# Earlier places for the second batch's keys, queries and values, and the strided heads' buffer as two tiles: one Trainium2 kernel, one change

## The chip, the cores and the metric

One core of one Trainium2 chip runs the whole program. The metric is the device time of one execution in microseconds, as the median of several runs. Beside it there is one profiled execution, from which all views below come. Engines: PE (matrix products), DVE and POOL (elementwise), ACT (activations and copies), SP (here it only issues transfers).

## The reference

Eight batches, eight heads, 576 positions, head size 64. Heads 0 to 3 see the last 32 positions; heads 4 to 7 see the earlier positions of the same residue modulo 32. Then a low-rank mix over the positions (U, V of rank 32) and a two-layer block with a ReLU:

```
scores = scale * q @ k.T ; masked by (0 <= i-j < 32) for heads 0-3,
                           by (i >= j and i % 32 == j % 32) for heads 4-7
attn   = softmax(scores) ; x = concat_heads(attn @ v)          # [8, 576, 512]
u      = x + (x.T @ U @ V).T
out    = u + relu(u @ w_ch1) @ w_ch2                           # 512 -> 2048 -> 512
```

U, V, w_ch1 and w_ch2 arrive as 64-bit floats.

## The kernel before

The two layers run as nine blocks of 512 columns (eight batches of 512 positions each, and one block of the eight remainders of 64). Each block has 16 steps (`fc`), each with 12 matmuls of 128x512 of the first layer (`gemm1`, L431) and 12 of the second (`gemm2`, L449): every float32 operand is split in a high and a low part (`uh`, `ul`; `gh`, `gl`; two halves of each weight `w`), and three of the four products are made. `gh` is made on ACT (L437), `gl` on DVE (L438).

The 64-bit weights come as 32 pieces (`raw`) and are converted while the first block runs. I call one piece a chunk: ACT L84, then DVE L86, L87 and L89, then ACT L112, then POOL L113.

Batch 0's attention runs ahead of the first block (`first_attention`). Beside block n runs the attention of batch n+1, step by step, after a plan with due times (`plan`, `tick`). Batches 0 and 1 do all eight heads on PE, as four pairs of heads; from batch 2 on, two pairs are on PE and the four strided heads run on POOL and DVE (`strided_heads`, tile `st`: queries in one half, keys and later values in the other).

One pair (`attention_pair`) is: scores (L143, L149 on PE), maximum and difference (DVE L157, L158), exp (ACT L161), transposes (PE L171), copy to `PT` (ACT L174), outputs (PE L182), normalisation (DVE L191 to L201: for a local pair its last piece is L196, for a strided pair L201). Then `mix_t` (PE L319, L323; ACT L326; DVE L328), `u_strided_early` (PE L386 and L359), `u_local` (L367, L359) and `u_tail` (L397, L359). From the first block on, all of these take their PSUM from one pool with one buffer, `px`:

```
    def psx2():
        banks["n"] += 1
        if banks["prefix"] and banks["n"] % 3:
            return ps_acc.tile([128, 2, 512], F32, name="acc")
        return ps_x.tile([128, 2, 512], F32, name="px")
```

Keys and queries (`kT`, `qT`) lie in the pool `att` of seven buffers, which `cv` (chunks), `s_sb`, `PT` and others share; values lie in one buffer `vt`. The code gives an order of emission; a scheduler then decides each engine's order with its own estimates of time, and every engine works through its own order strictly. All transfers go through SP's queue, where each waits for the one eight places ahead of it.

Of the kernel before, what the change touches and what calls it, by code (L numbers as in the profile page):

```python
# [7 lines left out]
F32 = mybir.dt.float32  # L8
# [10 lines left out]
NCH = S // 32  # L19
# [7 lines left out]
STAGGER = 3  # L27
ATT_BUFS = 7
PAIR_ORDER = (0, 2, 3, 1)
CHUNK_ORDER = ((2, 3, 0, 1), (0, 1, 2, 3))  # L30


@with_exitstack
def fused_kernel(ctx, tc, lqk, lv, eqk, ev, sqkv, U, V, wts, masks, eye, out):
# [10 lines left out]
    def att(shape, name, dtype=F32):  # L45
        return ap_.tile(shape, dtype, name=name, tag="att", bufs=ATT_BUFS)
# [11 lines left out]
    def dma(out, in_):  # L58
        last_dma[0] = nc.sync.dma_start(out=out, in_=in_).ins
# [35 lines left out]
    def load_weights(n):  # L95
        while wl["loaded"] < min(n, len(chunks)):
            k = wl["loaded"]
            c = chunks[k]
            raws[c] = const.tile([128, 512], I64, name="raw%d_%d_%d" % c, tag=wtag(*c))
            with tc.issue_after(last_dma[0]):  # L100
                dma(out=raws[c], in_=wts[k])
            wl["loaded"] += 1
# [12 lines left out]

    Vp = ap_.tile([96, S], F32R, name="Vp", tag="st")
    raw_u = att([128, 320], "raw_u", I64)
    raw_v = ap_.tile([32, S], I64, name="raw_v", tag="vt")  # L120

# [119 lines left out]
    o_str = {}  # L241

    def strided_heads(b):
        st = ap_.tile([128, 2, NCH * D], F32, name="st", tag="st")
        sq, sk = (st[:, x].rearrange("p (i d) -> p i d", d=D) for x in range(2))
        dma(out=st[:, 0], in_=sqkv[b - NSP, 0])
        dma(out=st[:, 1], in_=sqkv[b - NSP, 1])
        yield
        s_st = ap_.tile([128, NCH, NCH], F32, name="s_st")
        nc.gpsimd.memset(s_st, 8.0 * NEG)  # L250
        late = []

        def flush(n):
            while len(late) > n:
                late.pop(0)()

        for i in range(NCH):
            for j0 in range(0, i + 1, 9):
                n = min(9, i + 1 - j0)
                tmp = att([128, 9, D], "tmp")  # L260
                nc.gpsimd.tensor_tensor(out=tmp[:, 0:n], in0=sk[:, j0:j0 + n], in1=sq[:, i:i + 1].broadcast_to([128, n, D]),  # L261
                                        op=ALU.mult)
                late.append(lambda tmp=tmp, n=n, i=i, j0=j0: nc.vector.tensor_reduce(  # L263
                    out=s_st[:, i, j0:j0 + n], in_=tmp[:, 0:n], axis=AX.X, op=ALU.add))
                flush(1)
                yield
        flush(0)
        sv = sk
        dma(out=st[:, 1], in_=sqkv[b - NSP, 2])
        yield  # L270
        m_st = ap_.tile([128, NCH], F32, name="m_st")
        nc.vector.tensor_reduce(out=m_st, in_=s_st, axis=AX.X, op=ALU.max)
        nc.vector.tensor_tensor(out=s_st, in0=s_st, in1=m_st.broadcast_to([128, NCH, NCH]), op=ALU.subtract)
        nc.scalar.activation(out=s_st, in_=s_st, func=AF.Exp, scale=0.125)
        yield
        yield
        nc.vector.tensor_reduce(out=m_st, in_=s_st, axis=AX.X, op=ALU.add)
        nc.vector.tensor_scalar(out=m_st, in0=m_st, scalar1=1e-9, scalar2=None, op0=ALU.add)
        nc.vector.reciprocal(out=m_st, in_=m_st)
        nc.vector.tensor_tensor(out=s_st, in0=s_st, in1=m_st.broadcast_to([128, NCH, NCH]), op=ALU.mult)  # L280
        yield
        for i in range(NCH):
            step = D if i < 9 else D // 2
            for d0 in range(0, D, step):
                tmp = att([128, (i + 1) * step], "tmp")
                tv = tmp.rearrange("p (j d) -> p j d", d=step)
                nc.gpsimd.tensor_tensor(out=tv, in0=sv[:, 0:i + 1, d0:d0 + step],  # L287
                                        in1=s_st[:, i, 0:i + 1].broadcast_to([128, i + 1, step]), op=ALU.mult)
                late.append(lambda tv=tv, i=i, d0=d0, step=step: nc.vector.tensor_reduce(  # L289
                    out=sq[:, i, d0:d0 + step], in_=tv.rearrange("p j d -> p d j"), axis=AX.X, op=ALU.add))  # L290
                flush(1)
                yield
        flush(0)
        yield
        xT = st[:, 1].rearrange("p (e s) -> p e s", e=2)
        nc.vector.transpose(out=xT.rearrange("p e (i r) -> p i e r", r=32), in_=sq.rearrange("p i (e x) -> p i e x", x=32))
        o_str[b] = xT
        yield
        for h in range(4):
            rows = slice(32 * h, 32 * h + 32)  # L300
            xh = x_str.rearrange("p t (e h x) -> p t h e x", e=2, h=4)[:, :, h]
            oh = sq[rows].rearrange("p i (e x) -> p i e x", e=2)
            for i4 in range(4):
                nc.scalar.copy(out=xh[32 * i4:32 * i4 + 32, 0:4], in_=oh[:, i4:16:4])  # L304
                if i4 % 2:
                    yield
            for i4 in range(2):
                nc.scalar.copy(out=xh[32 * i4:32 * i4 + 32, 4], in_=oh[:, 16 + i4])
            yield
# [174 lines left out]
    def run_staggered(gens, lag):  # L484
        live, waiting, n = [], list(gens), 0
        while live or waiting:
# [5 lines left out]
                    live.remove(g)  # L492
            yield

    def first_attention():
        scratch = [up.tile([128, NDC * TB], F32, name="scr", tag=t) for t in ("uh", "ul")]
        late = [const.tile([128, 9, D + 1], F32, name=f"ve{n}", tag=wtag(n // 4, 3, n % 4)) for n in range(8)]
        loads = {}

        def load(k):  # L500
            pr = PAIR_ORDER[k]
            if k < 3:
                qk = [scratch[j // 3][:, S * (j % 3):S * (j % 3) + S] for j in (2 * k, 2 * k + 1)]
            else:
                qk = [att([128, S], "kT"), att([128, S], "qT")]
            loads[k] = pair_loads(0, pr, (*qk, late[2 * k], late[2 * k + 1]))

        load(0)
        dma(out=masks_sb, in_=masks)
        dma(out=ident, in_=eye)  # L510
        load(1)
        load(2)
        small_loads()
        load(3)
        load_weights(24)
        nc.gpsimd.memset(x_loc[64:128, 4], 0.0)
        nc.gpsimd.memset(x_str[64:128, 4], 0.0)
        pairs = [attention_pair(0, pr, loads[k]) for k, pr in enumerate(PAIR_ORDER)]
        beside = {3: lambda: (small_u(), small_v()), 4: lambda: convert(2)}
        seen = 0  # L520
        steps = run_staggered(pairs, STAGGER)

        def go(n):
            nonlocal seen
            for _ in range(n):
                if next(steps, "end") == "end":
                    return
                if len(exps) > seen:
                    seen = len(exps)
                    beside.get(seen, lambda: None)()  # L530

        go(3 * STAGGER + 8)
        mix_t(0, 1)
        go(2)
        u_strided_early(0, 2)
        go(40)
        mix_t(0, 0)
        u_strided_early(0, 3)
        for dc in range(2):
            u_local(0, (dc,))  # L540
        convert(5)

    first_attention()
    banks["prefix"] = False
    load_weights(32)
    pend = []
    c0 = wl["conv"]

# [5 lines left out]
    def task(gen, key, start, rate=1.0, after=()):  # L554
        return [gen, key, start, rate, after, 0.0]
# [6 lines left out]
    def plan(n):  # L562
        b = n + 1
        if n == 0:
            return [
                task(calls(lambda: u_tail(0)), "tail0", 2),
                task(run_staggered([attention_pair(1, pr) for pr in (2, 3, 0, 1)], 7), "pairs", 2, 1.0),
                task(calls(lambda: mix_t(1, 1), lambda: mix_t(1, 0)), "mix", 30, 0.4, ("pairs",)),
                task(calls(lambda: u_strided_early(1, 2), lambda: u_strided_early(1, 3), lambda: u_local(1, (0, 1)),
                           lambda: u_tail(1)), "u", 38, 0.34, ("mix",)),  # L570
            ]
        if b < B:
            return [
                task(strided_heads(b), "str", 0, 1.5),
                task(run_staggered([attention_pair(b, 0), attention_pair(b, 1)], 5), "pairs", 0, 1.0),
                task(calls(lambda: mix_t(b, 0)), "mix0", 20, 1.0, ("pairs",)),
                task(calls(lambda: u_local(b, (0, 1))), "u0", 26, 1.0, ("mix0",)),
                task(calls(lambda: mix_t(b, 1)), "mix1", 47, 1.0, ("str",)),
                task(calls(lambda: u_strided(b), lambda: None, lambda: None, lambda: u_tail(b)), "u1", 53, 1.0, ("mix1", "u0")),
            ]  # L580
        if b == B:
            return [task(u_rest(), "rest", 12)]
        return []
# [116 lines left out]
```

## Time and profile before

| what | us |
|---|---|
| median of 3 runs | 953.71 |
| lowest and highest | 951.01, 954.39 |
| the profiled execution | 954.11 |
| its span in the trace | 952.3 |
| PE, DVE, ACT, POOL busy | 917.1, 536.9, 247.3, 403.4 |

The time of the profiled execution is 1.8 us above the span of its trace. In the profile, L431 is line 431 of the kernel before; in the kernel after the change the lines up to 480 stand two further down (L431 is L433, L182 is L184). A row of a timeline has the start, the length, the engine, the line, the operation, output <- inputs, and in brackets the idle time before it with what ended it. Matmuls overlap, so the lengths of two neighbours add up to more than the time that they take.

### The profile page before, as it was taken

To read this page: it belongs to the slowest core of one execution; us is meant where nothing else is said; L and a number is where in the kernel's file an instruction comes from. 1 tells how busy PE (TensorE), PEld (TensorE's weight loads), DVE (VectorE), ACT (ScalarE), POOL (GpSimd) and SP (SyncE) were. 2 spreads that over 40 slices of the span, in tenths; PEclk is the share of its full clock that TensorE was granted. 3 is DMA by queue.
4 is the path that set the end of the run, shared out by engine and by line. 5 is a ranking of instruction groups with operands and counts; after the bars stand their busy time and mean duration, and the time that the engine had idled before them with its cause. 6 is when DMAs were issued, how large, how long until landed. Compare 5 with 4: busy or idle time off the path is not lost.

```text
span 952.3 us, 16503 instructions
## 1 busy us (share of the span) xinstructions
PE 917.1 (96%) x6896; PEld 725.8 (76%) x6896; DVE 536.9 (56%) x912; ACT 247.3 (26%) x486; POOL 403.4 (42%) x407
## 2 busy tenths in 40 slices
PE   5789898999999999999999999999999999999998
PEld 3557566878787787778778878787778788888886
DVE  4686778548936693659465964597448831112112
ACT  2443345212421142114311341115112521111110
POOL 0142233565639471939185816763575530002000
PEclk9989998999999999999999999999999999999999
DMA  9962202111022101220122003110210020001001
GB/s 338 408 259 67 77 27 75 45 57 52 25 79 71 52 26 56 70 76 5 41 105 77 1 25 119 33 51 26 95 56 26 1 80 15 1 1 45 1 1 44
DMA packets 27098, 64.50 MB, mean 68 GB/s; under 512 B 6768, under 2 KB 7280, under 8 KB 27024
## 3 DMA queue, kind: packets, MB, share of 16 engines
q1 hardware_dynamic: 27024, 63.45, 19.2%
q8 instruction: 54, 0.88, 0.4%
q14 instruction: 20, 0.16, 0.1%
HBM read 52.96 MB, written 10.49 MB: 67 GB/s over the span
## 4 chain that ended last, share of the span: by engine, by line
PE 79%; issue 9%; DVE 4%; POOL 3%; DMA 3%; ACT 0%; SPq 0%; POOLq 0%; DVEq 0%
PE ph L431 37%; PE acc L449 36%; POOL w L113 3%; DVE st L289 2%; DMA raw<-in_wts_dram 2%; PE px L182 1%; PE px L149 1%; PE px L359 1%; PE px L171 1%; DMA ve<-in_ev_dram 1%; PE px L319 1%; PE acc L462 1%; PE px L367 1%; DMA masks_sb<-in_masks_dram 0%; DVE ta L328 0%
## 5 line engine op out<-in xcount | busy, mean ns | idle before, releaser
L431 PE MATMUL ph<-uh,w 128*128 128x512 f32 x1152 | 393.3, 401 | 10.1 <-ACT w L112 5.1
L449 PE MATMUL acc<-gh,w 128*128 128x512 f32 x1136 | 375.4, 392 | 2.2 <-ACT gh L437 1.5
L431 PEld LDWEIGHTS ph<-uh,w 128*128 128x128 f32 x1152 | 217.9, 191 | 62.0 <-ACT w L112 6.7
L449 PEld LDWEIGHTS acc<-gh,w 128*128 128x128 f32 x1136 | 212.7, 188 | 49.0 <-ACT gh L437 2.3
L438 DVE SCALAR_TENSOR_TENSOR gl<-ph,gh 128x512 fp32r<-128x512 f32 x144 | 99.0, 689 | 239.6 <-ACT gh L437 239.0
L431 PE MATMUL ph<-ul,w 128*128 128x512 f32 x576 | 228.7, 398 | 0.0
L449 PE MATMUL acc<-gl,w 128*128 128x512 f32 x568 | 222.4, 392 | 0.0
L261 POOL TENSOR_TENSOR tmp<-st 128x576 f32<-128x576 f32 (+6 forms) x162 | 166.2, 1070 | 88.5 <-DMA st<-in_sqkv_dram 45.4
L437 ACT ACTIVATE gh<-ph 128x512 fp32r<-128x512 f32 x144 | 85.7, 597 | 365.2 <-PE ph L431 341.3
L287 POOL TENSOR_TENSOR tmp<-st,s_st 128x448 f32<-128x448 f32 (+7 forms) x162 | 135.5, 875 | 59.1 <-DVE s_st L280 59.1
L289 DVE TENSOR_REDUCE st<-tmp 128x64 f32<-128x64 f32 (+8 forms) x162 | 133.6, 882 | 1.2 <-POOL tmp L287 0.9
L431 PEld LDWEIGHTS ph<-ul,w 128*128 128x128 f32 x576 | 109.9, 191 | 23.5 <-DVE ul L351 0.6
L449 PEld LDWEIGHTS acc<-gl,w 128*128 128x128 f32 x568 | 106.8, 188 | 22.9 <-issue 0.4
L263 DVE TENSOR_REDUCE s_st<-tmp 128x9 f32<-128x576 f32 (+6 forms) x162 | 87.9, 566 | 44.3 <-POOL tmp L261 44.1
L113 POOL TENSOR_TENSOR w<-cv,w 128x512 fp32r<-128x512 f32 x32 | 43.6, 1369 | 99.2 <-ACT w L112 92.7
L479 POOL TENSOR_TENSOR o<-o,uh 128x512 f32<-128x512 f32 x32 | 40.7, 1297 | 92.8 <-DVE o L478 92.8
L351 POOL TENSOR_TENSOR ul<-st,uh 128x1024 fp32r<-128x1024 f32 x6 | 14.4, 2399 | 103.4 <-ACT uh L350 103.4
L304 ACT COPY x_str<-st 32x256 f32<-32x256 f32 x96 | 38.8, 404 | 36.2 <-DVE st L289 35.0
L87 DVE SCALAR_TENSOR_TENSOR cv<-raw,cv 128x512 int32<-128x512 int32 x32 | 28.4, 892 | 0.4
L112 ACT CAST w<-cv 128x512 fp32r<-128x512 f32 x32 | 19.7, 620 | 31.2 <-DVE cv L89 26.4
L89 DVE SCALAR_TENSOR_TENSOR cv<-raw,cv 128x512 int32<-128x512 int32 x32 | 27.4, 862 | 0.4
L161 ACT ACTIVATE s_sb<-s_sb 128x640 f32<-128x640 f32 x20 | 14.8, 740 | 49.2 <-DVE s_sb L158 49.1
(117 smaller groups left out, 504.4 us busy)
## 6 DMA issues: line engine op xcount, KB each, us to landing
raw<-in_wts_dram SPq DMA_DIRECT2D x32, 512.0 KB, 10.2
st<-in_sqkv_dram SPq DMA_DIRECT2D x18, 576.0 KB, 4.9
out_dram<-o SPq DMA_DIRECT2D x35, 256.0 KB, 2.0
vt<-in_lv_dram SPq DMA_DIRECT2D x14, 585.0 KB, 3.8
kT<-in_lqk_dram SPq DMA_DIRECT2D x15, 288.0 KB, 2.7
qT<-in_lqk_dram SPq DMA_DIRECT2D x15, 288.0 KB, 3.1
ve<-in_lv_dram SPq DMA_DIRECT2D x4, 292.5 KB, 6.0
ve<-in_ev_dram SPq DMA_DIRECT2D x4, 292.5 KB, 5.5
```

The costliest lines, as they stand in the source:

```text
L87: nc.vector.scalar_tensor_tensor(out=i, in0=hi_w, scalar=-0x80000000, in1=i, op0=ALU.bitwise_and, op1=ALU.bitwise_or)
L113: nc.gpsimd.tensor_tensor(out=parts[:, 1], in0=f, in1=parts[:, 0].bitcast(F32), op=ALU.subtract)
L261: nc.gpsimd.tensor_tensor(out=tmp[:, 0:n], in0=sk[:, j0:j0 + n], in1=sq[:, i:i + 1].broadcast_to([128, n, D]), op=ALU.mult)
L263: late.append(lambda tmp=tmp, n=n, i=i, j0=j0: nc.vector.tensor_reduce(out=s_st[:, i, j0:j0 + n], in_=tmp[:, 0:n], axis=AX.X, op=ALU.add))
L287: nc.gpsimd.tensor_tensor(out=tv, in0=sv[:, 0:i + 1, d0:d0 + step], in1=s_st[:, i, 0:i + 1].broadcast_to([128, i + 1, step]), op=ALU.mult)
L289: late.append(lambda tv=tv, i=i, d0=d0, step=step: nc.vector.tensor_reduce(out=sq[:, i, d0:d0 + step], in_=tv.rearrange("p j d -> p d j"), ...
L304: nc.scalar.copy(out=xh[32 * i4:32 * i4 + 32, 0:4], in_=oh[:, i4:16:4])
L431: nc.tensor.matmul(ph, w_parts[0, g, dc][:, part, fs], ut[:, dc, :], start=(k == 0 and i == 0), stop=(k == NDC - 1 and i == 2))
L437: gate[:] = [nc.scalar.activation(out=gh, in_=ph, func=AF.Relu).ins]
L438: nc.vector.scalar_tensor_tensor(out=gl, in0=ph, scalar=0.0, in1=gh.bitcast(F32), op0=ALU.max, op1=ALU.subtract)
L449: nc.tensor.matmul(accs[n][m // 2][:, m % 2], w_parts[1, g, f][:, part, ms], gt, start=(fc == 0 and i == 0), stop=(fc == NFC - 1 and i == 2))
L479: nc.gpsimd.tensor_tensor(out=o, in0=o, in1=uh[:, m].bitcast(F32), op=ALU.add)
```

## The change

The keys and queries of batch 1's first three pairs get the places that batch 0's had (`scr`, in the buffers `uh` and `ul` that the first block does not use), and its values get two places, `vt` and the strided heads' second half, `st1`. The pairs are numbered in a list of their own. The loads are issued where the plan's first task starts, with due time 0, and the last weight loads come after three of them. The strided heads' buffer becomes two tiles, `st0` (queries, results) and `st1` (keys, values, the transposed result).

```diff
+SECOND_ORDER = (2, 3, 0, 1)
+SECOND_STAGGER = 7
...
-    Vp = ap_.tile([96, S], F32R, name="Vp", tag="st")
+    Vp = ap_.tile([96, S], F32R, name="Vp", tag="st0")
...
     def strided_heads(b):
-        st = ap_.tile([128, 2, NCH * D], F32, name="st", tag="st")
-        sq, sk = (st[:, x].rearrange("p (i d) -> p i d", d=D) for x in range(2))
-        dma(out=st[:, 0], in_=sqkv[b - NSP, 0])
-        dma(out=st[:, 1], in_=sqkv[b - NSP, 1])
+        st = [ap_.tile([128, NCH * D], F32, name=f"st{x}") for x in range(2)]
+        sq, sk = (z.rearrange("p (i d) -> p i d", d=D) for z in st)
+        for x in range(2):
+            dma(out=st[x], in_=sqkv[b - NSP, x])
...
-        dma(out=st[:, 1], in_=sqkv[b - NSP, 2])
+        dma(out=st[1], in_=sqkv[b - NSP, 2])
...
-        xT = st[:, 1].rearrange("p (e s) -> p e s", e=2)
+        xT = st[1].rearrange("p (e s) -> p e s", e=2)
...
+    scratch = [up.tile([128, NDC * TB], F32, name="scr", tag=t) for t in ("uh", "ul")]
+    places = [scratch[j // 3][:, S * (j % 3):S * (j % 3) + S] for j in range(6)]
+    second_v = {}
+    def second_qk(k):
+        pr = SECOND_ORDER[k]
+        src = lqk[1, pr] if pr < 2 else eqk[1, pr - 2]
+        qk = places[2 * k:2 * k + 2] if k < 3 else [att([128, S], "kT"), att([128, S], "qT")]
+        for place, x in zip(qk, src):
+            dma(out=place, in_=x)
+        return (*qk, lambda c: second_v[k][:, c])
+    def second_values(k):
+        pr = SECOND_ORDER[k]
+        second_v[k] = ap_.tile([128, NCH, D + 1], F32, name="vt", tag="st1" if k % 2 else "vt")
+        dma(out=second_v[k].rearrange("p c x -> p (c x)"), in_=lv[1, pr] if pr < 2 else ev[1, pr - 2])
+    def second_attention():
+        loads = []
+        for k in range(3):
+            loads.append(second_qk(k))
+            if k < 2:
+                second_values(k)
+        load_weights(len(chunks))
+        loads.append(second_qk(3))
+        pairs = [attention_pair(1, pr, loads[k]) for k, pr in enumerate(SECOND_ORDER)]
+        steps, n = run_staggered(pairs, SECOND_STAGGER), 0
+        for _ in steps:
+            n += 1
+            if n in (8, 8 + SECOND_STAGGER):
+                second_values(2 + (n > 8))
+            yield
...
     first_attention()
     banks["prefix"] = False
-    load_weights(32)
...
-                task(run_staggered([attention_pair(1, pr) for pr in (2, 3, 0, 1)], 7), "pairs", 2, 1.0),
+                task(second_attention(), "pairs", 0, 1.0),
```

What the scheduler makes of it, at three places. First SP's queue behind the 28th weight chunk (before) and the 24th (after); `scr` are keys and queries in their new places, `raw` the last weights, `rest` a store. Before:

```order
L59 DMA vt<-in_ev_dram 128x1170
L59 DMA raw_3_0_697<-in_wts_dram 128x512
L59 DMA raw_3_1_699<-in_wts_dram 128x512
L59 DMA raw_3_2_701<-in_wts_dram 128x512
L59 DMA raw_3_3_703<-in_wts_dram 128x512
L59 DMA rest<-tl 512x1x64
L59 DMA kT<-in_eqk_dram 128x576
L59 DMA qT<-in_eqk_dram 128x576
```

After:

```order
L61 DMA scr<-in_eqk_dram 128x576 x4
L61 DMA vt<-in_ev_dram 128x1170
L61 DMA scr<-in_lqk_dram 128x576 x2
L61 DMA raw_3_2_714<-in_wts_dram 128x512
L61 DMA raw_3_3_716<-in_wts_dram 128x512
L61 DMA raw_3_0_718<-in_wts_dram 128x512
L61 DMA raw_3_1_720<-in_wts_dram 128x512
L61 DMA vt<-in_ev_dram 128x1170
```

Six keys and queries and one load of values moved ahead of the last eight weight chunks; the fourth pair's keys and queries stand behind them, as all four pairs' did.

Second, PE from the outputs of batch 1's fourth pair to its first `mix_t`. Before, with the first 7 of the 28 rows that lie between:

```order
L182 MATMUL px<-vt,PT 32x65 x36
L449 MATMUL acc<-gh,w_2_1_1403 128x512 x2
L449 MATMUL acc<-gl,w_2_1_1403 128x512
L449 MATMUL acc<-gh,w_2_1_1403 128x512 x3
L449 MATMUL acc<-gl,w_2_1_1403 128x512
L449 MATMUL acc<-gh,w_2_1_1403 128x512
L449 MATMUL acc<-gh,w_2_2_1431 128x512
L449 MATMUL acc<-gl,w_2_2_1431 128x512
```

After, with all that lies between:

```order
L184 MATMUL px<-vt,PT 32x65 x36
L433 MATMUL ph<-uh,w_2_0_1334 128x512
L433 MATMUL ph<-uh,w_2_1_1366 128x512
L433 MATMUL ph<-ul,w_2_1_1366 128x512
L433 MATMUL ph<-uh,w_2_0_1334 128x512
L433 MATMUL ph<-uh,w_2_1_1366 128x512
L433 MATMUL ph<-ul,w_2_1_1366 128x512
L433 MATMUL ph<-uh,w_2_1_1366 128x512 x2
L321 MATMUL px<-x_str,U_sb 32x256 x4
```

`mix_t` stands 8 product matmuls behind the outputs, where it stood 37 behind. In the same way the third pair's scores stand 12 behind the second pair's outputs (24 before), the transposes 3 behind the scores in the fourth pair, and the whole attention of batch 1 ends earlier in the block, counted in product matmuls: fourth outputs at the 208th (256th before), first `mix_t` at the 216th (293rd), second `mix_t` at the 249th (300th), `u_strided_early` at the 278th and 304th (304th and 312th), `u_local` at the 312th (346th).

Third, DVE at the normalisation of that fourth pair (`rt`, `x_loc`), which reads `px`; `cv` rows are weight chunks. Before:

```order
L191 TENSOR_SCALAR rt<-px 128x2x4
L89 SCALAR_TENSOR_TENSOR cv<-raw_3_2_689,cv 128x512
L192 RECIPROCAL rt<-rt 128x2x4
L86 TENSOR_SCALAR cv<-cv 128x512
L196 TENSOR_TENSOR x_loc<-px,rt 128x2x4x64
```

After:

```order
L193 TENSOR_SCALAR rt<-px 128x2x4
L91 SCALAR_TENSOR_TENSOR cv<-raw_2_1_162,cv 128x512
L194 RECIPROCAL rt<-rt 128x2x4
L88 TENSOR_SCALAR cv<-cv 128x512
L198 TENSOR_TENSOR x_loc<-px,rt 128x2x4x64
L193 TENSOR_SCALAR rt<-px 64x2
L89 SCALAR_TENSOR_TENSOR cv<-raw_2_2_164,cv 128x512
L194 RECIPROCAL rt<-rt 64x2
L91 SCALAR_TENSOR_TENSOR cv<-raw_2_2_164,cv 128x512
L198 TENSOR_TENSOR x_loc<-px,rt 64x128
```

The pieces of the normalisation stand among the chunks as they did before; the chunks are earlier ones (of the third quarter of the weights, where they were of the fourth).

More of the change, by code (lines that the diff above doesn't have):

```diff
@@ L493, in run_staggered @@
             yield
+    scratch = [up.tile([128, NDC * TB], F32, name="scr", tag=t) for t in ("uh", "ul")]
[27 more added lines that the diff above has]
+            yield
     def first_attention():
-        scratch = [up.tile([128, NDC * TB], F32, name="scr", tag=t) for t in ("uh", "ul")]
         late = [const.tile([128, 9, D + 1], F32, name=f"ve{n}", tag=wtag(n // 4, 3, n % 4)) for n in range(8)]
@@ L502, in load @@
             if k < 3:
-                qk = [scratch[j // 3][:, S * (j % 3):S * (j % 3) + S] for j in (2 * k, 2 * k + 1)]
+                qk = places[2 * k:2 * k + 2]
             else:
```

## Prediction

> **What bounds the kernel now.** First the page, for the span; then the table by stage, for where PE is not full; then PE's own waits in that stage; then the clock.
>
> ```profile
> span 952.3 us, 16503 instructions
> ```
> ```profile
> 42.00:78.00 36.00, 31.80 (x185) 23.42 (x186) 28.81 (x41) 16.90 (x32) 10.60 (x8) 0.91 0.64 245
> 78.00:108.00 30.00, 28.16 (x326) 21.01 (x325) 19.12 (x40) 11.84 (x20) 9.62 (x8) 1.00 0.23 71
> 108.00:127.00 19.00, 13.41 (x255) 8.85 (x255) 11.87 (x23) 7.09 (x12) 4.78 (x4) 0.91 0.17 49
> 127.00:145.00 18.00, 18.00 (x149) 14.53 (x148) 14.58 (x25) 7.36 (x13) 6.54 (x5) 1.00 0.10 34
> 145.00:179.00 34.00, 30.32 (x153) 22.79 (x152) 24.89 (x39) 15.37 (x29) 15.26 (x15) 0.90 0.16 53
> 179.00:279.00 100.00, 100.00 (x743) 79.65 (x742) 63.41 (x103) 26.39 (x55) 51.98 (x52) 1.00 0.17 52
> ```
>
> Columns: stretch, length, then busy time of PE, PEld, DVE, ACT, POOL, the granted clock, DMA. From 179 us on PE is full (100.00 of 100) and nothing the change does there can be worth more than PE's few waits. The first block (42 to about 179 us) is where PE waits, and only there does the change move PE's order much. From 78 to 179 PE idles 1.84 + 5.59 + 0 + 3.68 = 11.1 us, and in 0.09 x 19 and 0.10 x 34 us of lost clock another 5.1 us go: 16.2 us in all. That is the most a better order could win there. Some of its named causes (us in all, times, longest):
>
> ```profile
> PE ph L431 <- ACT w L112: 3.6, 2, 2.0
> PE px L386 <- DVE ta L328: 1.2, 1, 1.2
> PE px L171 <- ACT s_sb L161: 1.0, 1, 1.0
> PE px L182 <- ACT PT L174: 0.8, 1, 0.8
> ```
>
> No DMA is among PE's waits. The transfers that the change frees did wait in SP's queue, mostly for outputs to release the values' place (64 to 166 us):
>
> ```profile
> SPq L59 <- PE px L182: 49.5, 4, 18.8
> ```
>
> So loading keys, queries and values earlier shortens no wait of PE by itself. It lets the scheduler place the second batch's attention earlier in PE's order, and the price is read there. PE's pace between waits is 2.72/12 = 0.227 us a matmul of the two products:
>
> ```profile
> 814.76 2.72 PE acc L449 x12
> ```
>
> **The change part by part.** PE's work is the same 24 x 144 product matmuls and four pairs; only waits differ. The pairs share one PSUM tile, px: scores, transposed scores, outputs and mix_t each need the one before it read out. I call first to fourth the second batch's four pairs.
>
> *Fourth pair to mix_t.* Between that pair's outputs and mix_t stood 37 product matmuls; now 8 (the order above). What has to happen between is DVE's normalisation, the last piece of which stands behind conversion chunks:
>
> ```profile
> 131.77 0.64 ACT L174 COPY PT<-px 128x576 f32<-128x576 f32 x1 [1.12 <-PE px L171]
> ...
> 136.13 0.98 PE L182 MATMUL px<-vt,PT 64*32 64x65 f32 x72
> ...
> 144.39 0.28 DVE L196 TENSOR_TENSOR x_loc<-px,rt 64x128 f32<-64x128 f32 x1
> ```
>
> From the end of PT's copy (132.41) to the end of the normalisation (144.67) went 12.3 us, with four chunks and one gl in DVE's way; no wait of mix_t for it is among PE's, since its 37 matmuls covered it. In the new order the same chain again holds four chunks (ACT starts the next chunk only behind PT's copy, as before) and no gl, 0.7 us by its row below: 11.6. PE's cover is 0.1 to start, 0.98 of outputs and 8 x 0.227 = 1.8: 2.9. **Wait 8.7.** Bounds: a chunk (2.3 us, below) fewer in the way, 6.4; one more, 11.0. Only a normalisation that runs ahead of its chunks would take it to nothing (the first rival). Part may show as a wait for the converted weights w, which the same chain makes.
>
> *Second pair to third pair's scores.* Between stood 24 matmuls; now 12.
>
> ```profile
> 96.81 0.64 ACT L174 COPY PT<-px 128x576 f32<-128x576 f32 x1 [3.71 <-PE px L171]
> ...
> 100.33 0.98 PE L182 MATMUL px<-vt,PT 64*32 64x65 f32 x72
> ...
> 106.62 0.35 DVE L201 TENSOR_TENSOR x_str<-px,rt 64x64 f32<-64x64 f32 x2
> ```
> ```profile
> L87 DVE SCALAR_TENSOR_TENSOR cv<-raw,cv 128x512 int32<-128x512 int32 x30 | 27.0, 905 | 0.3
> L89 DVE SCALAR_TENSOR_TENSOR cv<-raw,cv 128x512 int32<-128x512 int32 x30 | 26.0, 873 | 0.4
> L86 DVE TENSOR_SCALAR cv<-cv 128x512 int32<-128x512 int32 x30 | 14.9, 503 | 14.3 <-ACT cv L84 14.3
> L438 DVE SCALAR_TENSOR_TENSOR gl<-ph,gh 128x512 fp32r<-128x512 f32 x16 | 10.8, 684 | 3.7 <-ACT gh L437 3.5
> ```
>
> There the same chain, 97.45 to 106.97, was 9.5 us with three chunks and a gl. A chunk is 0.905 + 0.873 + 0.503 = 2.3 us of DVE in the mean. The new order has two chunks and the rest of an earlier one (about 2.4), and no gl: 9.5 - 0.7 - 0.6 x 2.3 = 7.4. Cover: 0.1 + 0.98 + 12 x 0.227 = 3.8. **Wait 3.6**, bounds 1.3 (a chunk fewer) and 5.7 (the chain as long as before).
>
> *Transposes.* Scores to transposes is a chain of reduce, subtract and exp. The third pair before:
>
> ```profile
> 111.76 0.86 PE L171 MATMUL px<-ident,s_sb 128*128 128x128 f32 x5 [0.96 <-ACT s_sb L161]
> 113.41 0.98 PE L182 MATMUL px<-vt,PT 64*32 64x65 f32 x72 [0.78 <-ACT PT L174]
> ```
>
> Six matmuls lay between there, and 0.96 was left. The second pair has 12 now (nothing left, but outputs right behind the transposes: 0.8 again), the fourth has 3: 0.96 + 3 x 0.227 = 1.7, and 0.5 for the chunk that its next product needs, which starts behind the subtract. **3.0 together.**
>
> *After mix_t.* Here the new order is better: mix_t's halves stand 33 matmuls apart instead of 7, the next user 29 behind; L386's wait for ta (1.2) has cover. One place is worse: u_local stood 34 matmuls behind the second u_strided_early, now 8. What lies between is what lay between the two u_strided_early before, also 8 matmuls apart:
>
> ```profile
> 154.90 0.85 PE L359 MATMUL px<-Vp,tst 96*128 96x512 f32 x2
> 155.78 1.09 ACT L350 CAST uh<-px 128x512 fp32r<-128x512 f32 x1
> ...
> 157.48 1.11 DVE L351 TENSOR_TENSOR ul<-px,uh 128x512 fp32r<-128x512 f32 x1
> ...
> 159.12 1.01 PE L386 MATMUL px<-ident,x_str 128*128 128x128 f32 x5
> ```
>
> 155.75 to 159.12 is 3.4, less 1.8 of cover: **1.5**, from 0 (PE late anyway) to 6 (two more chunks ahead on DVE).
>
> *Clock.* A cluster of waits is followed by half clock:
>
> ```profile
> 115.00:118.60 3.60, 1.61 (x8) 0.86 (x7) 3.56 (x9) 0.63 (x2) 0.80 (x2) 1.00 0.55 169
> 118.60:122.00 3.40, 3.26 (x8) 2.15 (x7) 1.08 (x4) 0.62 (x1) 2.36 (x2) 0.50 0.00 0
> ```
>
> PE was idle 2.0 us of 3.6 and then ran 3.4 us at 0.50. The new waits (3.6 and 8.7, and a cluster at the end) are as many such places as the old, so I keep the old price, **5.1**; from 2.5 to 8. [...]
>
> *Start of the block.* The first pair's scores move ahead of u_tail(0). Their keys and queries now stand behind 24 weight transfers, and ahead of the last eight:
>
> ```profile
> raw<-in_wts_dram SPq DMA_DIRECT2D x24, 512.0 KB, 10.2
> ```
>
> A transfer took 10.2 us to land with eight in flight; the slots are issued at 41.4 and 42.6, so they land near 52, when PE gets there; PE idled at this place before too (4.2 us of 42:78). DVE's reduce and subtract, 1.65 us, now stand ahead of the first gl, but are not to be done later. I take 0, from -1 to +2. The last eight weights land seven smaller transfers later, less than another 10.2 us, and are needed only for the last quarter of the block: 0.
>
> *Strided heads in two tiles.* In blocks 1 to 6 PE's only wait is this one:
>
> ```profile
> PE px L323 <- ACT x_str L308: 0.6, 2, 0.4
> ```
> ```profile
> st<-in_sqkv_dram SPq DMA_DIRECT2D x18, 576.0 KB, 4.9
> ```
>
> Queries no longer wait for the tile that the previous batch's tail reads, so the keys load alone; with one load behind the tail where there were two, the strided chain starts sooner, by a part of those 4.9 us. PE is full, so the gain is those **0.6**.
>
> Sum for the first block: 8.7 + 3.6 + 3.0 + 1.5 + 5.1 = 21.9, against the 16.2 it replaces: +5.7. Less 0.6: +5.1. The profiled execution took 954.1 (span 952.3 and 1.8 around it), 0.4 above the median 953.7: 959.2 for it, **958.8** against the median.
>
> **The rivals.** *The waits do not come (faster).* If POOL's and DVE's chunks run ahead, so that the normalisations follow the outputs at once, the px waits go, and the earlier attention only spreads the work: 3.0 and one clock drop (1.7) stay of 16.2, -11.5 and -0.6: 941.6. For it: DVE idles 14.3 us on ACT's first conversion step in this block. Against: those steps stand in ACT's order behind PT's copy of the very pair. It decides once fewer than about two chunks stand between outputs and normalisation.
>
> *The strided chain becomes the bound (slower still).* PE reaches the L323 of each block two matmuls sooner (0.45 us), and the 0.6 shows that chain to be level with PE. If the two tiles do not shorten it, or POOL's new order lengthens it by a microsecond, five or six blocks pay 0.5 to 1 each: 958.8 + 4 = 963. Against: one load fewer behind the tail.
>
> *No difference.* If both px waits fall a chunk short and u_local finds PE late: 6.4 + 1.3 + 3.0 + 0 + 5.1 = 15.8 against 16.2, less 0.6: 952.7. For it: every term is of the size of what it replaces; against: both errors would have to lie on one side.
>
> **How the numbers follow.** Forecast (953 to 965): 0.50; waits do not come: 0.20; strided bound: 0.15; no difference: 0.15. Half a per cent, 4.8 us, is about what a measurement of this kernel can tell from no change. The forecast's own range lies with 0.27 above 958.5 and 0.23 within; the first rival 0.18 faster, 0.02 within; the second slower; the third within. Faster 0.18, same 0.40, slower 0.42. The range 945 to 966 leaves out half of the first rival and a third of the second.
>
> **What would show it.** Right: PE's waits in the first block name L321 and L145 on DVE's normalisation (L198, L203), one of 7 to 10 us about 10 us behind the fourth pair's scores, and a clock of 0.5 behind it; PE full from the second block on; no wait of PE on a DMA. Wrong: PE's idle time from 78 us to the block's end under 8 us, clock 1.00 in slices 3 to 7; then the chunks were not in the way. L325 waits of over 0.5 us in each block would show the strided rival.

## The result, and the profile after

| | median us | ratio to before, 95% interval |
|---|---|---|
| before (5 runs beside the kernel after) | 951.01 | |
| after (5 runs) | 960.44 | 1.0091 [1.0063, 1.0118] |

The kernel after is slower by 0.9%. Its profiled execution took 960.4 us with a span of 958.7, 6.4 above the span of before. The two medians differ by more, 9.4, since the kernel before came out at 951.01 in these runs; it took 952.7 to 953.5 in the larger sets of the experiments below. The table by stage of the kernel after, with the columns as in the prediction (stretch, length, busy time of PE, PEld, DVE, ACT, POOL, granted clock, DMA):

```profile
42.00:78.00 36.00, 31.04 (x260) 23.51 (x261) 26.73 (x46) 16.84 (x32) 10.80 (x8) 0.91 0.80 309
78.00:108.00 30.00, 25.39 (x308) 19.24 (x307) 22.73 (x40) 12.33 (x21) 7.92 (x7) 0.89 0.07 22
108.00:127.00 19.00, 15.81 (x266) 11.19 (x264) 10.00 (x19) 6.52 (x11) 5.86 (x5) 0.91 0.18 56
127.00:145.00 18.00, 12.40 (x69) 9.11 (x70) 11.43 (x22) 5.51 (x13) 5.22 (x4) 0.81 0.02 9
145.00:179.00 34.00, 29.91 (x128) 23.76 (x127) 28.14 (x41) 15.90 (x29) 18.12 (x16) 0.90 0.11 35
179.00:279.00 100.00, 100.00 (x743) 79.84 (x742) 63.14 (x102) 26.00 (x55) 51.92 (x52) 1.00 0.15 49
```

As before, PE is full from the second block on. Between 78 and 179 us it idles 17.5 us (11.1 before), and 11.8 us of clock are lost (5.1 before): the same sum as in the prediction, 0.11 x 30 + 0.09 x 19 + 0.19 x 18 + 0.10 x 34. PE's own waits from 40 to 200 us (engine and line, released by; us in all, times, longest):

```profile
PE px L321 <- DVE x_loc L198: 5.6, 1, 5.6
PE px L369 <- ACT tl L394: 4.1, 1, 4.1
PE px L145 <- DVE x_str L203: 3.9, 1, 3.9
PE ph L433 <- ACT w L114: 2.7, 3, 1.5
PE px L173 <- ACT s_sb L163: 1.7, 1, 1.7
PE px L151 <- DMA scr<-in_eqk_dram: 1.5, 1, 1.5
...
PE px L184 <- ACT PT L176: 0.7, 1, 0.7
```

The three largest are waits on px that before did not have. Counting the matmuls of the two products in the trace gives where the time goes: with 100 of them behind it the next starts at 80.2 us (78.9 before), with 150 at 102.1 (95.3), with 216 at 134.6 (126.0); the 384th, the last of the first block, starts at 186.9 (179.3), the last of all at 954.7 (948.3). So 7.6 us are lost by the end of the first block, and 1.2 come back in the blocks behind it, where the wait on `x_str` is gone.

How the largest wait comes about is seen in the timeline (start, length, line, operation) of the fourth pair's outputs on PE, of DVE from there to the end of the normalisation, and of PE behind it:

```profile
123.24 1.24 PE L184 MATMUL px<-vt,PT 64*32 64x65 f32 x72
...
125.81 1.45 DVE L88 TENSOR_SCALAR cv<-cv 128x512 int32<-128x512 int32 x1
127.30 1.65 DVE L89 SCALAR_TENSOR_TENSOR cv<-raw,cv 128x512 int32<-128x512 int32 x1
128.87 0.15 DVE L193 TENSOR_SCALAR rt<-px 128x8 f32<-128x8 f32 x1
128.98 0.69 DVE L91 SCALAR_TENSOR_TENSOR cv<-raw,cv 128x512 int32<-128x512 int32 x1
...
130.66 1.61 DVE L89 SCALAR_TENSOR_TENSOR cv<-raw,cv 128x512 int32<-128x512 int32 x1
132.19 0.15 DVE L194 RECIPROCAL rt<-rt 64x2 f32<-64x2 f32 x1
132.30 0.69 DVE L91 SCALAR_TENSOR_TENSOR cv<-raw,cv 128x512 int32<-128x512 int32 x1
132.91 0.28 DVE L198 TENSOR_TENSOR x_loc<-px,rt 64x128 f32<-64x128 f32 x1
```
```profile
133.33 1.08 PE L321 MATMUL px<-x_str,U_sb 128*32 128x256 f32 x8 [5.56 <-DVE x_loc L198]
```

The outputs end at 124.48, and the first piece of the normalisation starts 4.4 us later, behind chunk operations. The normalisation needs some 1.6 us of DVE (its six pieces), and is spread over 4.3, its pieces standing between those of the chunks. The clock around the waits (columns as in the table by stage):

```profile
86.00:89.90 3.90, 1.82 (x8) 1.05 (x6) 3.90 (x9) 0.62 (x1) 1.56 (x2) 1.00 0.34 128
89.90:96.90 7.00, 5.19 (x82) 3.83 (x83) 6.15 (x14) 3.47 (x6) 2.03 (x2) 0.51 0.01 2
...
120.60:124.00 3.40, 2.76 (x58) 1.92 (x64) 1.64 (x4) 2.27 (x4) 1.28 (x1) 0.53 0.00 0
124.00:130.80 6.80, 3.06 (x47) 1.66 (x31) 6.73 (x12) 3.42 (x6) 3.46 (x3) 0.98 0.26 88
130.80:137.70 6.90, 4.37 (x23) 3.16 (x24) 6.05 (x12) 2.21 (x6) 2.19 (x2) 0.52 0.01 2
161.60:165.00 3.40, 0.04 (x1) 0.00 (x0) 3.33 (x5) 2.75 (x5) 1.58 (x2) 1.00 0.77 287
165.00:171.80 6.80, 6.08 (x19) 5.03 (x20) 6.80 (x11) 3.68 (x7) 5.46 (x6) 0.51 0.00 0
```

Each of the three long waits is followed by 6.8 us at half clock, which begin while PE still waits; the wait of 1.7, with one of 0.9 behind it, by 3.4. From 78 us on that is 23.9 us at half clock, 10.2 before. The length of the longest wait alone does not tell which. In the kernel before 6.8 us followed waits of 1.6 us at most:

```profile
149.30:152.70 3.40, 1.41 (x16) 0.70 (x7) 3.31 (x6) 2.20 (x5) 1.28 (x1) 1.00 0.00 0
152.70:159.50 6.80, 5.92 (x17) 4.40 (x18) 6.67 (x10) 4.53 (x9) 2.69 (x2) 0.50 0.32 89
```

PE idled 2.0 of 3.4 us there, and 0.9 more in the stretch at half clock. In the kernel after the stretches of 6.8 us have 0.5 to 2.3 us of waiting in them, that of 3.4 has 0.4. In a later run (mix_t later, below) the same wait of 3.9 us stood in a stretch (78 to 108 us) with a granted clock of 0.94, where the kernel after had 0.89: by these 1.8 us of clock were lost in place of 3.3. So waits of one length came with two prices here; what sets the price was not shown.

### The profile page after: what moved, and what is told of

Same layout as the page of the kernel before. It is cut to its first block, busy times and chain, and to the rows that moved or that the text cites. A ratio compares the mean times of both kernels' runs of the same rounds, so it can differ in the third digit from the quotient of the medians.

```text
span 958.7 us, 16511 instructions
## 1 busy us (share of the span) xinstructions
PE 914.6 (95%) x6896; PEld 726.4 (76%) x6896; DVE 541.6 (56%) x912; ACT 246.9 (26%) x486; POOL 404.9 (42%) x407
## 4 chain that ended last, share of the span: by engine, by line
PE 88%; DMA 5%; DVE 4%; issue 1%; ACT 0%; SPq 0%; DVEq 0%; ACTq 0%
PE ph L433 40%; PE acc L451 40%; DMA raw<-in_wts_dram 3%; DVE cv L89 1%; PE px L151 1%; PE px L184 1%; PE px L361 1%; PE px L173 1%; PE px L321 1%; DVE cv L91 1%; DVE cv L88 1%; PE px L369 1%; DMA qT<-in_lqk_dram 1%; DMA scr<-in_lqk_dram 1%; DMA ve<-in_ev_dram 1%
## 5 line engine op out<-in xcount | busy, mean ns | idle before, releaser
L433 PE MATMUL ph<-uh,w 128*128 128x512 f32 x1152 | 387.2, 397 | 4.2 <-ACT w L114 2.7
L451 PE MATMUL acc<-gh,w 128*128 128x512 f32 x1136 | 382.3, 394 | 0.5 <-ACT gh L439 0.5
L263 POOL TENSOR_TENSOR tmp<-st,st 128x576 f32<-128x576 f32 (+6 forms) x162 | 167.6, 1071 | 85.4 <-DMA st<-in_sqkv_dram 37.0
L115 POOL TENSOR_TENSOR w<-cv,w 128x512 fp32r<-128x512 f32 x32 | 43.7, 1371 | 99.7 <-ACT w L114 98.4
L89 DVE SCALAR_TENSOR_TENSOR cv<-raw,cv 128x512 int32<-128x512 int32 x32 | 28.9, 909 | 0.4
L91 DVE SCALAR_TENSOR_TENSOR cv<-raw,cv 128x512 int32<-128x512 int32 x32 | 28.2, 886 | 0.3
## 6 DMA issues: line engine op xcount, KB each, us to landing
raw<-in_wts_dram SPq DMA_DIRECT2D x32, 512.0 KB, 10.2
```

The costliest lines, as they stand in the source:

```text
L89: nc.vector.scalar_tensor_tensor(out=i, in0=hi_w, scalar=-0x80000000, in1=i, op0=ALU.bitwise_and, op1=ALU.bitwise_or)
L115: nc.gpsimd.tensor_tensor(out=parts[:, 1], in0=f, in1=parts[:, 0].bitcast(F32), op=ALU.subtract)
L433: nc.tensor.matmul(ph, w_parts[0, g, dc][:, part, fs], ut[:, dc, :], start=(k == 0 and i == 0), stop=(k == NDC - 1 and i == 2))
L451: nc.tensor.matmul(accs[n][m // 2][:, m % 2], w_parts[1, g, f][:, part, ms], gt, start=(fc == 0 and i == 0), stop=(fc == NFC - 1 and i == 2))
```

## Experiments

My theory was that the new waits come from the normalisation standing behind weight chunks on DVE, on the single tile px. The rivals: that the two tiles or the transfers cost, that a short distance in PE's order costs whatever DVE does, or that the conversion of the weights binds, and px only shows where. Each ratio is against the kernel before, run on the same chip; medians of before were 952.7 to 953.5 there.

**The two tiles alone.** The kernel before with `st0` and `st1`:

```diff
-        st = ap_.tile([128, 2, NCH * D], F32, name="st", tag="st")
+        st = [ap_.tile([128, NCH * D], F32, name=f"st{x}") for x in range(2)]
```

> The kernel before with the strided heads' buffer as two tiles and nothing else; its PE order in the first block is the old one within two or three matmuls. My theory: worth the 0.6 us of the strided heads' one wait on PE, so 950.4 against 951.0, the wait of the x_str product on ACT gone. Rival (the two tiles hurt the strided chain from the second block on, 0.5 to 1 us a block): 954 to 957, with waits of PE on x_str in each block.

Measured: 953.17, ratio 0.9994 [0.9979, 1.001]. The wait on `x_str` is gone from PE's waits behind the first block; what is left there is the last block's 0.4 us. A gain of 0.6 us is too small for the ratio, and fits it; a loss of 3 us or more doesn't. The first block's waits are those of before. So the loss lies in the other part.

**Short chunks, in both kernels.** `to_f32` returns behind L88 (L86 before) for weight chunks:

```diff
         nc.vector.tensor_scalar(out=i, in0=i, scalar1=3, scalar2=None, op0=ALU.logical_shift_left)
+        if n == 512:
+            return f
```

> The kernel after, with two of the three integer operations of each weight chunk on DVE left out (the weights are then not the right ones), so that a chunk takes 0.5 us of DVE in place of 2.3; PE's order in the first block is the same within a few matmuls (fourth outputs at 208, mix_t at 216, third scores at 120). Theory (the new waits are the normalisation standing behind chunks on DVE): the waits of 5.6 (mix_t on x_loc), 3.9 (third scores on x_str) and 4.1 (u_local) fall under 1, under 1 and under 1.5, and at least three of the half-clock stretches (about 1.7 us each) go: 960.4 - 11 - 5 = 944, 940 to 949. Rival (a short distance in PE's order on the single px tile waits whatever DVE does): mix_t still waits 3 us or more, and the time stays above 953.

> The kernel before with the same two operations of each weight chunk left out. Theory: its own waits go as well (those for converted weights and gl, 10 us together in the first block, and most of the 5 us of lost clock), so 939 to 945; and without the chunks the change costs nothing: the difference of the two shortened kernels is within 3 us either way, where the full ones differ by 9.4. Rival (the order itself costs): the shortened kernel after stays 6 us or more above this one.

Measured: after 936.06, ratio 0.9822 [0.9807, 0.9838]; before 942.1, ratio 0.9873 [0.9855, 0.989]. With full chunks the change costs 0.9%, with short ones it gains 0.5%: more than the "within 3 us" of my theory. PE's waits in the shortened kernel after (its lines stand two further down):

```profile
PE px L175 <- ACT s_sb L165: 2.2, 2, 1.7
PE px L323 <- DVE x_loc L200: 1.9, 1, 1.9
...
PE px L147 <- DVE x_str L205: 0.6, 1, 0.6
```

The waits of 5.6, 3.9 and 4.1 are 1.9, 0.6 and gone; I had expected the first under 1. Its normalisation runs in one piece once it starts, but behind two L88 that took 2.5 us together beside POOL. The third pair's scores and mix_t stand in PE's order where they stood (behind 120 and 216 product matmuls), so that these two waits can be compared. u_local can't: it moved from behind 312 to behind 330, and has 28 matmuls of cover in place of 8. So this order is a good one where chunks are short, and full chunks turn it into a loss: this is shown for the kernels as a whole, and by wait for those two.

**u_local later.** In the plan of the first block:

```diff
-lambda: u_tail(1)), "u", 38, 0.34, ("mix",)),
+lambda: u_tail(1)), "u", 44, 0.34, ("mix",)),
```

> The kernel after with a later due time for batch 1's u steps: in PE's order the second u_strided_early moves from the 304th to the 312th product matmul and u_local from the 312th to the 342nd (30 behind instead of 8), nothing ahead of them moves. Theory: the 4.1 us wait of u_local goes, and with it the half clock that follows it (1.7 us): 954.6, 953 to 957. Rival (the chunk conversion is the bound there, and PE only waits for it at another place, as a wait for w): 959 to 961.

Measured: 961.2, ratio 1.0083 [1.0063, 1.0103]: no gain, and the rival's figure. Its waits:

```profile
...
PE ph L433 <- ACT w L114: 3.8, 3, 2.7
PE acc L451 <- ACT gh L439: 2.0, 2, 1.8
...
PE px L388 <- ACT tl L394: 1.2, 1, 1.2
```

The 4.1 us of u_local came back as 1.1 more for w, 1.5 more for gh and 1.2 at u_strided_early, and the granted clock from 145 to 179 us was 0.90 as in the kernel after (3.4 us lost). Here the conversion binds: in the kernel after, the last chunk's cast ends at 171.6 us (168.4 before), and PE could not go far ahead of it. A wait that is taken away by itself, in a stretch where the weights are as late, is handed on.

**mix_t later, and the pairs further apart.** Two ways to lengthen distances. In the first only mix_t and what follows is held back (`pe_last` is the latest matmul of the first layer that was emitted):

```diff
-task(calls(lambda: mix_t(1, 1), lambda: mix_t(1, 0)), "mix", 30, 0.4, ("pairs",)),
+task(calls(lambda: behind(lambda: mix_t(1, 1)), lambda: mix_t(1, 0)), "mix", 42, 1.0, ("pairs",)),
...
+    def behind(fn):
+        with tc.issue_after(pe_last[0]):
+            fn()
```

> The kernel after with the first mix_t of batch 1 held back behind a later product matmul: it stands 27 behind the fourth outputs in place of 8, the second mix_t and the u steps come later with it; nothing ahead of it moves. Theory of the distances: 4.3 of the 5.6 us wait of mix_t on x_loc and the 4.1 of u_local go, 950 to 954. Rival (the conversion binds here: the casts of the chunks that the next products need end at 130.4 and 133.7 us in the kernel after, and the wait ended at 133.3): PE waits for w in place of px, 957 to 961.

Measured: 954.24, ratio 1.0023 [1.0007, 1.004], at the edge of what the theory of the distances forecast. PE's waits:

```profile
PE px L145 <- DVE x_str L203: 3.9, 1, 3.9
PE ph L434 <- ACT w L114: 3.6, 2, 2.7
PE acc L453 <- ACT gh L441: 3.4, 2, 2.9
...
PE ph L434 <- DVE gl L442: 1.7, 1, 1.7
```

The 3.9 us of the third scores are untouched, those of mix_t and u_local are gone, and 5.0 us more of waits for w, gh and gl (0.5 each for gh and gl in the kernel after) have come in their place. Both theories hold in part: the time fell by some 6 us (the medians' difference; its profiled execution was the fastest of its runs, 950.8, and shows a larger gain).

In the second, the pairs start further apart:

```diff
-SECOND_STAGGER = 7
+SECOND_STAGGER = 9
```

> The kernel after with the pairs of batch 1 started 9 steps apart in place of 7. Places and loads are the same; in PE's order the third scores stand 27 product matmuls behind the second outputs (12 in the kernel after), mix_t 35 behind the fourth outputs (8), u_local 27 behind the second u_strided_early (8). Theory of the distances (a short distance on px is what costs): the waits of 3.9, 5.6 and 4.1 go with most of their half clock, 942 to 950. Rival (moving one wait only hands it to the chunk conversion, as in the kernel with later u steps): 955 to 961, with waits for w in their place.

Measured: 948.85, ratio 0.9973 [0.9957, 0.9988], faster than before by 0.3%. All three long px waits are gone, on a normalisation and at u_local. In their place stand 3.5 us more for gh, 0.4 more for w, and 1.6 of the second mix_t behind the first:

```profile
PE acc L451 <- ACT gh L439: 4.0, 3, 3.2
PE ph L433 <- ACT w L114: 3.1, 2, 1.6
...
PE px L321 <- DVE ta L330: 1.6, 1, 1.6
```

**The attention later, with the early places.** The steps start six idle steps behind the loads:

```diff
         loads.append(second_qk(3))
+        for _ in range(6):
+            yield
```

> The kernel after with six idle steps between the loads and the first pair: the transfers keep their early order, but the attention of batch 1 stands about where it stood in the kernel before (first outputs at the 88th product matmul, third outputs and fourth scores at 198 and 216, fourth outputs at 269, mix_t 35 behind). Theory (the early order of the attention costs, not the places or the transfers): 948 to 954, as before. Rival (the seven transfers ahead of the last eight weights, or the places, cost): 957 to 961, with the last chunks' conversion waiting for DMA.

Measured: 949.81, ratio 0.9979 [0.9966, 0.9992]. With the attention about where it was, but all places and early transfers kept, the loss is gone; no wait of PE on a DMA is in its table. So the transfers and places cost nothing that can be seen in the time; it was the order. (The 0.2% below before has no experiment of its own.)

**The chunk's last subtraction on DVE.** POOL's L115 overlaps DVE's chunk operations (20 of them started while it ran in the kernel after, the longest of 1.78 us):

```diff
-nc.gpsimd.tensor_tensor(out=parts[:, 1], in0=f, in1=parts[:, 0].bitcast(F32), op=ALU.subtract)
+nc.vector.tensor_tensor(out=parts[:, 1], in0=f, in1=parts[:, 0].bitcast(F32), op=ALU.subtract)
```

> The kernel after with the last subtraction of each weight chunk on DVE in place of POOL. In the kernel after a chunk's second or third integer operation on DVE takes 1.65 us where it coincides with POOL's subtraction and 0.69 where it doesn't. Theory (the two engines slow each other): with POOL silent a chunk is 0.4 + 0.7 + 0.7 + 0.7 = 2.5 us of DVE including its subtraction, no operation takes over 1 us, and the conversion is done sooner: 950 to 957. Rival (the long operations have another cause): 1.65 us operations remain, and DVE's added 0.7 us a chunk makes it 965 or more.

> The kernel before with the last subtraction of each weight chunk on DVE in place of POOL. Theory (the change's loss comes from a conversion that is slowed and stands in the way, so it goes with the slowing): this kernel gains less than the kernel after did, 945 to 950 where that came to 948.6, so that the two differ by 4 us at most, in place of 9.4. Rival (the move to DVE is worth the same in both, some 12 us): 939 to 942, and the loss of the change stays at 8 us or more.

Measured: after 948.59, ratio 0.9971 [0.9955, 0.9987], under the 950 that I had expected at the least; before 946.96, ratio 0.9952 [0.9934, 0.997]. By the medians the kernel after gains some 12 us, that of before less than 6, and the two differ by 1.6 us in place of 9.4. DVE's groups between 78 and 179 us (count, busy us, mean ns, idle us before), the kernel after first, then with the subtraction on DVE:

```profile
L89 DVE SCALAR_TENSOR_TENSOR cv<-raw,cv 128x512 int32<-128x512 int32 x22 | 20.3, 932 | 0.3
L91 DVE SCALAR_TENSOR_TENSOR cv<-raw,cv 128x512 int32<-128x512 int32 x22 | 19.0, 869 | 0.2
L88 DVE TENSOR_SCALAR cv<-cv 128x512 int32<-128x512 int32 x22 | 11.5, 529 | 6.2 <-ACT cv L86 6.2
```
```profile
L115 DVE TENSOR_TENSOR w<-cv,w 128x512 fp32r<-128x512 f32 x22 | 15.5, 709 | 0.8 <-ACT w L114 0.3
L91 DVE SCALAR_TENSOR_TENSOR cv<-raw,cv 128x512 int32<-128x512 int32 x22 | 14.9, 687 | 0.1
L89 DVE SCALAR_TENSOR_TENSOR cv<-raw,cv 128x512 int32<-128x512 int32 x22 | 14.8, 684 | 0.1
L88 DVE TENSOR_SCALAR cv<-cv 128x512 int32<-128x512 int32 x22 | 9.0, 418 | 2.9 <-ACT cv L86 2.9
```

A chunk of three operations took 932 + 869 + 529 = 2.3 us of DVE; with the subtraction added, 709 + 687 + 684 + 418 = 2.5. DVE does a fourth operation for 0.2 us more, and POOL's 1.37 us (the mean of 32) behind the cast are gone. The wait of mix_t fell from 5.6 to 1.5. PE's order moved a little too, in both kernels (in that of after the third pair's scores from behind 120 products to behind 141, in that of before the second pair's from 122 to 145), so not all of the gain is DVE's pace.

**Both edits.** The 9 steps, and the six idle steps, each with the subtraction on DVE:

> The kernel after with both edits that gained: pairs 9 steps apart, and the last subtraction of a chunk on DVE. Theory: the waits that the 9 steps left (w 3.1, gh 4.0) shrink with the faster conversion, 940 to 946, below either alone (948.9, 948.6). Rival (both take away the same waits): 947 to 950.

> The kernel after with six idle steps ahead of the first pair and the last subtraction of a chunk on DVE. Theory: the later attention leaves waits for w, gl and POOL's part (7.5 us together), and the faster conversion takes half of them: 943 to 947. Rival (what is left is the chain of reduce, exp and transposes, and the clock): 948 to 950.

Measured: 945.95, ratio 0.9936 [0.9915, 0.9956]; and 943.68, ratio 0.9913 [0.9893, 0.9934], the fastest of those that do all the work, 9 us under before. The kernel before with the same subtraction took 946.96, so that some 3 of the 9 us come with the change and its idle steps. The longest waits that are left are on the conversion, in the chain of one pair, and of the second mix_t behind the first:

```profile
PE ph L433 <- ACT w L114: 3.0, 2, 1.5
PE px L173 <- ACT s_sb L163: 2.5, 1, 2.5
PE px L321 <- DVE ta L330: 2.3, 1, 2.3
```

## Why the prediction was right, and where it wasn't

- **The mechanism was right.** Earlier transfers took no wait of PE away, since before had none on a DMA; the earlier order brought the waits that were named (L321, L145, on DVE's normalisation), and the sign follows from the chunks, as the pair of shortened kernels shows.
- **Fourth pair to mix_t, 8.7: measured 5.6**, under the lower bound. The chain was sized right (from PT's copy at 121.7 to 133.2: 11.5 us, 11.6 forecast). The cover was not: in place of 2.9 us PE took 6.0 (121.7 to 127.8). Its outputs started 1.5 us behind PT's copy and not 0.1, since four product matmuls stood ahead of them; these and the outputs ran at a lower clock (0.53 granted from 120.6 to 124.0 us; the four 0.43 us apart, the outputs 1.24 us long in place of 0.98); and it waited 0.7 for w on the way.
- **Second pair to third scores, 3.6: measured 3.9.** Chain 83.5 to 91.65, 8.1 us against 7.4; cover 4.3 against 3.8.
- **Transposes, 3.0: measured 1.7 and 0.7**, and 0.9 for the next product's chunk, where 0.5 was forecast.
- **u_local, 1.5 from 0 to 6: measured 4.1**, since chunks stood on both engines of its chain, a cast ahead of `uh` and of `tl` on ACT, more than a chunk ahead of `ul` on DVE. But as a term of a sum it was wrong: by itself it was worth nothing that was measured, since the weights were as late.
- **Clock, 5.1 kept: measured 11.8.** This is the term that failed. I took one price for a cluster of waits; the trace shows stretches of 3.4 or of 6.8 us at half clock behind them, with 0.4 us of waiting inside the short one and 0.5 to 2.3 inside the long ones, and three of the four here were long ones. One followed each of the three waits of 3.9 to 5.6 us; in the kernel before, a long one followed waits of 1.6 us at most. No row stands behind the 2.5 at the lower end of my range.
- **Why the time came out near all the same: in part by luck.** The idle time in all, 16.8 forecast and 17.5 measured, is near since the first wait's error and u_local's cancel. By the same reading 17.5 + 11.8 = 29.3 us replaced 16.2, 13.1 more where 5.7 were forecast, but the block's end moved by 7.6 only. Three things were not in my sum. Of the 23.9 us at half clock some 4.5 lie inside the waits, where PE has nothing to do, so that idle time and clock count about 2.2 us twice. The small matmuls of the third pair's scores, at a granted clock of 0.50, took 1.31 us where the fourth's took 0.92 at 1.00, and not double. And the first pair's transposes and outputs, 0.86 + 0.98 us by the rows of the prediction, came behind 78 us before and ahead of it now. Their shares in the 5.5 us were not measured apart.

```profile
92.35 1.31 PE L151 MATMUL px<-scr 64*32 64x32 f32 x72
...
116.05 0.92 PE L151 MATMUL px<-kT,qT 64*32 64x32 f32 x72
```

- **Start of the block, 0: nearly so, but with a wait on a DMA that I had excluded.** The first scores waited 1.5 us for `scr` behind 24 weight transfers; the product matmul behind the 16th started at 52.9 us, 51.8 before. Behind the 50th nothing was left of it (66.4 and 66.5).
- **Strided heads, 0.6: the wait went.** Behind the first block the kernel after made up 1.2 us on that of before, and the kernel with the two tiles alone 0.9 (0.6 us behind that of before at the first block's end, 0.3 ahead at the last matmul). The rival that this chain becomes the bound fell with that.
- **The first rival (the waits do not come)** decides as it said, once the chunks are out of the way: 936.06 against 942.1, though 6 us and not 12.

## What to carry to other kernels

Before moving work earlier, count what will stand between two users of a single buffer, on every engine of the chain: here the distance in PE's order shrank while the DVE queue in between kept its length. Waits in a stretch whose real bound is another chain (here the conversion) are not a sum: taking u_local's 4.1 us away handed 3.8 on, and what gained was a faster chain (948.59) or an order with more slack throughout (948.85). And look at the engine next door: the cheapest microseconds here were in an operation on POOL beside which DVE's L89 took 932 ns in the mean, and 684 without it.

## What the runs showed of the hardware

DVE's two-input chunk operations (L89, L91) took 0.69 us alone, and up to 1.78 where POOL's subtraction was running when they started (L91 at 99.89). To L89 at 130.66 above, 1.61 us long, belongs this row:

```profile
130.45 1.26 POOL L115 TENSOR_TENSOR w<-cv,w 128x512 fp32r<-128x512 f32 x1 [2.06 <-ACT w L114]
```

POOL ends at 131.71 and L89 at 132.27. In the trace of the kernel after 16 operations of L89 and L91 started so, and each ended 545 to 551 ns behind POOL's, however long that still ran. The one-input L88 took longer too, 1.45 us at 125.81 in place of 0.42; its four that started so ended 283 to 287 ns behind POOL's. So in these 20 cases the end of the chunk operation went with POOL's end, 0.55 us (L89, L91) or 0.28 (L88) behind it, and its time was not stretched in proportion. Without POOL's subtraction the means of L91, L89 and L88 are 687, 684 and 418 ns, where they were 869, 932 and 529.

What that cost this kernel: moving POOL's subtraction to DVE added 0.2 us a chunk to DVE, and the kernel after became 12 us faster with it, part of which is the order that moved.
